# Spectral mixer and bilinear GLU on one core: products split out of their PSUM banks, weight sums on another engine, a new order at two seams

## The chip, the cores and the metric

One core of a Trainium2 chip. The metric is the device time of one execution in microseconds (us), lower is better; the kernel before took 715.27 us (median of three runs, 714.61 to 717.80).

## The reference

All of it is fp32, on a sequence of S = 2048 tokens of D = 640:

```python
h  = x + irfft2(rfft2(layernorm(x)) * (w_r + 1j*w_i))
z  = layernorm(h)
h2 = h + ((z @ w_gate) * (z @ w_up)) @ w_down      # F = 1728, no other nonlinearity
```

## The kernel before, in words

The first 194 us or so do the spectral part as matmuls with Fourier tables; the change does not touch them. The rest is the GLU, in two blocks of 1024 tokens. The 1728 columns of F are cut into 14 chunks of 128 (the last is half a chunk). A fp32 operand is split into a rounded high part, **hi** (written by ACT, ScalarE), and the rest, **lo** (source minus hi, written by VectorE = DVE or GpSimd = POOL); each product of two split operands is three matmuls: hi·hi, hi·lo, lo·hi. The accumulators `e` (gate and up) and `d` (down) are PSUM banks, four of each.

**Chunks.** A block starts with chunks 12 and 13, done plainly (`gu`, `gate_parts`: u copied by ACT, gate times up by DVE, then the split). Chunks 0 to 11 go in six *pairs* p = 0..5, chunk 2p (even) and 2p+1 (odd). `strassen` computes one chunk, gate and up over both halves of the tokens, by a Strassen scheme in seven products. I call them P1 to P7 in the order of the code; P1, P3 and P5 are 6 matmuls of 512 columns, P2, P4, P6 and P7 are 9. P1, P3, P5 and P7 go into bank `oa`, P2 and P4 into `ob`, P6 into `oc`. After P1, P2 and P3 ACT copies the bank to SBUF (`h0`, `c22`, `h1`; lines 971, 981, 985); DVE adds later banks to these copies (988, 991, 1004) and multiplies (992: `h1`; 1010: `h0`). So a chunk gives two finished tiles, `h0` and `h1`, gate times up for the two token halves.

**Down products.** The down projection of a finished pair is itself a Strassen scheme, over the four tiles of the pair (even chunk: a11 = `h0`, a21 = `h1`; odd chunk: a12 = `h0`, a22 = `h1`). It needs seven split operands, kept in `hop` (tile `ht`), slots 0 to 6: a11, a12, a22, a21+a22, a21+a22-a11, a11-a21 (`s3`), a12-(a21+a22-a11) (`s4`). `down_products` makes 28 products of 3 matmuls with 320 columns (84 in all), in ten groups g0 to g9 of 3, 3, 3, 2, 3 (twice over). Each is followed at once by a DVE addition to the output rows `x` (line 921). The first group holds p1a, p5a, p1b; the second p5b, p6a, p3a. p6a accumulates on the bank of p1a, so it waits until DVE has added p1a to `x`; p3a needs slot 6 (`s4`).

**Order.** It is written by hand. `strassen` calls `at(n)` behind product Pn; I say *slot n*. The groups of the pair before are hung into slots 2 to 7 of the even chunk (g0 to g5) and 1 to 4 of the odd one (g6 to g9), side jobs too. The next chunk's gate and up weights are prepared one chunk ahead (`prep`, `ahead[0..3]`: ACT copies 834 and 846, POOL rests 835 and 851, POOL sums 838 to 841), the down weights in five steps `wdn[0..4]` (`load_d`): `plain` at slot 3, `sums` at slot 6 and a further part at slot 7 of the even chunk, two more parts at slot 4 of the odd chunk. `sums` is four subtractions of 128x320 on DVE (588 to 591); the ACT copy of `wdn[2]` (line 580) waits for them.

Most of the change lies at the odd chunk's end. Behind P5 DVE adds to `c22`, multiplies `h1`, forms a21+a22 (995) and a21+a22-a11 (996) in SBUF, and `split` makes three lo's (939). Then come the additions and the product for `h0` (1004, 1010) and `s4` (1018). The splits of `s4` and `h0` (a12) are put off into the next chunk (`HELD["late"]`), behind its P1.

**Other pieces.** At a block's start chunks 12 and 13 run beside the preparation of the token sums (`t12`, `t34`), whose lo for `t3` is made by `lo()`, line 710. The first pair has the down products of chunks 12 and 13 in its slots instead (`down`, 10 matmuls for each j of 8: j = 0 to 3 in slots 2 to 5, two each in slots 6 and 7 of the even chunk; none in the odd one). In chunk 11 of the first block ACT also normalises the eight row tiles of the next block (line 645), all at slot 4.

Of the kernel before, what the change touches and what calls it, by code (L numbers as in the profile page):

```python
# [13 lines left out]
AF = mybir.ActivationFunctionType  # L14
OP = mybir.AluOpType

P = 128
# [21 lines left out]
def f32(ap):  # L39
    return ap.bitcast(F32)  # L40
# [29 lines left out]
def tile_spectral_glu(ctx: ExitStack, tc: tile.TileContext, x, wf, wgu, wlast, wdown, wdlast,  # L70
# [31 lines left out]
    def wk(shape, name):  # L102
        return work.tile(shape, F32, tag="wk", name=name)
# [464 lines left out]
    def load_d(p):  # L568
        w = home("dA" if p in (0, 2, 4) else "dB", [P, 2, 1280], "wd", F32R)
        raws = [wk([P, D], "draw") for _ in range(2)]  # L570
        if p >= 5:
            return split_in(("d", p), w, wdown[p] if p < 6 else wdlast, raws, nc.gpsimd)
        v = home("dC", [P, 2, 960], "wt", F32R)
        W["d", p] = w, v
        for i, r in enumerate(raws):
            nc.sync.dma_start(r, wdown[p][:, D * i:D * i + D])
        (r, q), sub = raws, OP.subtract

        def part(o, a, src, n):
            act(o[:, 0, a:a + n], src, AF.Copy)  # L580
            nc.gpsimd.tensor_tensor(o[:, 1, a:a + n], src, f32(o[:, 0, a:a + n]), op=sub)

        def plain():
            part(w, 0, r[:, 0:320], 320)
            part(w, 320, q, 640)

        def sums():
            tt(r[:, 0:320], r[:, 320:640], r[:, 0:320], op=sub)  # L588
            tt(r[:, 320:640], q[:, 320:640], r[:, 320:640], op=sub)
            tt(q[:, 320:640], q[:, 320:640], r[:, 0:320], op=sub)  # L590
            tt(q[:, 0:320], q[:, 0:320], q[:, 320:640], op=sub)
# [341 lines left out]

    HELD = {}

    def split(src, a, engine=None):
        hi, lo = (hop[:, a, l] for l in range(2))
        act(hi, src, AF.Copy)  # L938
        (engine or nc.vector).tensor_tensor(lo, src, f32(hi), op=OP.subtract)  # L939

    def strassen(c, blk, ahead, downs, side):
        wa, ws = W[c]
        p, odd = divmod(c, 2)

        def at(n):
            if downs.get(n):
                for f in downs[n]:
                    f()
                if c:
                    pop(1)  # L950
            for f in side.get(n, ()):
# [19 lines left out]
        act(h0, oa, AF.Copy)  # L971
# [19 lines left out]
        tt(c22, oa, c22, op=OP.add)  # L991
        tt(h1, h1, c22, op=OP.mult)  # L992
        if odd and p < 5:
            a11, a21 = HELD["a11"], HELD["a21"]
            tt(a21, a21, h1, op=OP.add)  # L995
# [3 lines left out]
        elif odd:  # L999
            split(h1, 4)  # L1000
        at(5)
        oc = single()
        product(oc, True, wa, 0, b21, [(wa, 256, b5[0])])
        tt(h0, oc, h0, op=OP.add)
        if ahead and not odd:
# [4 lines left out]
        tt(h0, oa, h0, op=OP.mult)  # L1010
        if not odd:
            HELD["a11"], HELD["a21"] = h0, h1
            if p < 5:
                nc.gpsimd.tensor_tensor(c22, h0, h1, op=OP.subtract)
                HELD["s3"] = c22
        elif p < 5:
            s4 = wk([P, 512], "s4")
            tt(s4, h0, c22, op=OP.subtract)
            HELD["late"] = [(s4, 6), (h0, 1)]
        at(7)  # L1020
        if c == 11:
            split(h0, 5)

    order = [6, 0, 1, 2, 3, 4, 5]
    steps = [(blk, p) for blk in range(2) for p in order]
# [1 line left out]
    for n, (blk, p) in enumerate(steps):  # L1027
        if p == 6:
            if blk == 0:
# [23 lines left out]
                hi, lo = t34(0)  # L1053
                hi()
                late()
                lo()
                wdn = load_d(p)
            else:
                copies, sums, high, low = prep(0, blk)
# [26 lines left out]
                    t_rest(j)  # L1086
                late()
                gu(NC - 1, 1)
                issue(wdn)
                for j in range(4):  # L1090
                    t1s[j][1]()
                late = gate_parts(NC - 1, 1)
                hi, lo = t34(0)
                hi()
                late()
                lo()
# [14 lines left out]
        wdn = load_d(p)  # L1111
        slots = [{}, {}]
        if prev[1] == 6:
            js = [[0], [1], [2], [3], [4, 5], [6, 7]]
            slots[0] = {n: [lambda j=j, prev=prev: down(*prev, j) for j in k] for n, k in enumerate(js, 2)}
        else:
            fs = down_products(*prev, (0, 1)) + down_products(*prev, (2, 3))
            slots[0] = dict(zip(range(2, 8), fs))
            slots[1] = dict(zip((1, 2, 3, 7 if p == 5 else 4), fs[6:]))
        for ci in range(2):  # L1120
            c = 2 * p + ci
            side = {n: [] for n in range(8)}
            ahead = None
            if c < 11:
                ahead = prep(c + 1, blk)
                if c < 10:
                    side[6 if ci else 7].append(lambda c=c: load_raw(c + 2))
            if p == 5:
                if ci == 0:
                    side[3].append(lambda wdn=wdn: issue(wdn))  # L1130
                else:
                    side[4].append(lambda: (split(HELD["a11"], 0, nc.gpsimd), split(HELD["a21"], 3)))
            elif ci == 0:
                side[3].append(wdn[0])
                side[6].append(wdn[1])
                side[7].append(wdn[2])
            else:
                def rest(wdn=wdn, ahead=ahead):
                    split(HELD["a11"], 0, nc.gpsimd)
                    ahead[2]()  # L1140
                    ahead[3]()
                    wdn[3]()
                    split(HELD["s3"], 5, nc.gpsimd)
                    wdn[4]()

                side[4].append(rest)
            if c == 11 and blk == 0:
                pop(len(fill))
                dj = load_direct(1, [wk([P, D], "draw"), stage[:, 0:640], stage[:, 640:1280]])
                side[1] += [lambda: issue(dj[0]), lambda: issue(dj[1]), lambda: load_raw(0)]  # L1150

                def low(ks):
# [142 lines left out]
```

## Time and profile before

| | us |
|---|---|
| runs: median (lowest to highest) | 715.27 (714.61 to 717.80) |
| the profiled execution, its own time | 717.91 |
| its span, first to last instruction | 716.0 |
| PE busy in the span | 687.9 (96%) |
| DVE / POOL / ACT busy | 539.5 / 363.2 / 312.1 |
| mean granted PE clock | 0.99 |

PE is busy 96% of the span, so the time is PE's work plus the gaps between its matmuls. In a timeline row the first number is the start from the span's start, the second how long the row lasts, then engine, line, output<-inputs and the count; in brackets stands the idle time ahead of it and what ended it. Matmuls overlap, so a group's true cost is read from one row's start to the next row's start, not from the duration.

### The profile page before, as it was taken

Reading aid. Unit: us, or ns where it says so; the run is one execution under the profiler, and the core shown is the slowest. Engines: PE = TensorE matmul, PEld = TensorE weight load, DVE = VectorE, ACT = ScalarE, POOL = GpSimd, SP = SyncE. Lnnn points to the kernel's source line nnn. Section 1 sums busy time; section 2 is a strip of 40 time slices with the busy share of each in tenths; the row PEclk is TensorE's granted clock in tenths of the full one; section 3 lists DMA queues with packets and bytes.
Section 4 is the critical chain, followed back from the end, with each engine's and each line's share of the span. In section 5 each row is a group of like instructions: output and inputs, shape, how many; then the busy total and the mean of one; then the engine's idle time right before and its main releaser. Section 6 shows DMA issues by size and latency. Waiting matters only on the chain.

```text
span 716.0 us, 10313 instructions
## 1 busy us (share of the span) xinstructions
PE 687.9 (96%) x3784; PEld 606.2 (85%) x3784; DVE 539.5 (75%) x1022; ACT 312.1 (44%) x605; POOL 363.2 (51%) x322
## 2 busy tenths in 40 slices
PE   8999999999999899999999999999799999999998
PEld 8989989887797688888888889888688888888888
DVE  7968886998866878787877667665778778686755
ACT  6966674475514234342425263433315243334310
POOL 3101114330368676768676714266766767768600
PEclk9999999999999999999999999999799999999999
DMA  9426771002211111121213113300212121211003
GB/s 336 174 94 201 229 224 52 0 1 75 74 37 42 38 44 63 38 73 38 75 37 92 38 43 148 105 8 30 74 38 74 38 74 38 74 38 57 18 1 148
DMA packets 21075, 55.07 MB, mean 77 GB/s; under 512 B 2336, under 2 KB 7200, under 8 KB 21024
## 3 DMA queue, kind: packets, MB, share of 16 engines
q1 hardware_dynamic: 20304, 52.53, 22.2%
q0 software_dynamic: 288, 1.48, 0.6%
q8 instruction: 30, 0.49, 0.3%
q10 hardware_dynamic: 432, 0.39, 0.2%
q14 instruction: 21, 0.17, 0.1%
HBM read 49.16 MB, written 5.24 MB: 76 GB/s over the span
## 4 chain that ended last, share of the span: by engine, by line
PE 69%; DVE 25%; ACT 3%; issue 2%; POOL 1%; DVEq 0%; ACTq 0%
PE e L109 32%; PE d L109 21%; DVE ht L939 5%; DVE h L995 2%; DVE h L992 2%; PE re L109 2%; PE im L109 2%; PE u L413 2%; PE im L455 2%; PE eo L109 2%; DVE c L996 2%; PE im L241 1%; PE re L282 1%; DVE c L991 1%; DVE h L1010 1%
## 5 line engine op out<-in xcount | busy, mean ns | idle before, releaser
L109 PE MATMUL e<-xt,wst 128*128 128x512 f32 x864 | 216.3, 395 | 0.0
L109 PEld LDWEIGHTS e<-xt,wst 128*128 128x128 f32 x864 | 162.2, 191 | 31.3
L109 PE MATMUL d<-wd,ht 128*128 128x320 f32 x832 | 147.7, 312 | 4.7 <-DVE ht L939 3.6
L921 DVE TENSOR_TENSOR x<-d,x 128x320 f32<-128x320 f32 x280 | 123.9, 483 | 37.6 <-PE d L109 33.4
L109 PEld LDWEIGHTS d<-wd,ht 128*128 128x128 f32 x832 | 131.6, 189 | 13.9 <-DVE ht L939 4.1
L835 POOL TENSOR_TENSOR wst<-raw,wst 128x1024 fp32r<-128x1024 f32 x23 | 55.3, 2406 | 99.0 <-ACT wst L834 83.0
L109 PE MATMUL d<-wt,ht 128*128 128x320 f32 x360 | 70.8, 314 | 13.0 <-DVE x L921 13.0
L109 PE MATMUL e<-t,wst 128*128 128x512 f32 x288 | 74.7, 395 | 0.9 <-ACT h L971 0.9
L109 PEld LDWEIGHTS d<-wt,ht 128*128 128x128 f32 x360 | 57.9, 189 | 17.8 <-DVE x L921 16.0
L851 POOL TENSOR_TENSOR wst<-raw,wst 128x896 fp32r<-128x896 f32 (+1 forms) x46 | 71.4, 1574 | 0.2 <-ACT wst L846 0.2
L109 PEld LDWEIGHTS e<-t,wst 128*128 128x128 f32 x288 | 53.0, 189 | 10.9 <-ACT h L971 1.5
L846 ACT ACTIVATE wst<-raw 128x896 fp32r<-128x896 f32 (+1 forms) x48 | 30.2, 677 | 45.7 <-POOL raw L840 44.9
L988 DVE TENSOR_TENSOR h<-e,h 128x512 f32<-128x512 f32 x24 | 16.6, 691 | 43.3 <-PE e L109 38.5
L938 ACT ACTIVATE ht<-h 128x512 fp32r<-128x512 f32 x48 | 29.8, 625 | 34.1 <-DVE h L992 19.0
L580 ACT ACTIVATE wd<-draw 128x320 fp32r<-128x320 f32 (+1 forms) x30 | 15.7, 558 | 66.2 <-DVE draw L588 66.2
L109 PE MATMUL e<-xt,wdir 128*128 128x512 f32 x180 | 42.1, 392 | 0.2 <-DVE ht L790 0.2
L484 POOL CAST qr<-bits 1x128 fp32r<-1x128 f32 x15 | 4.2, 280 | 71.4 <-DVE qr L488 71.4
L109 PEld LDWEIGHTS e<-xt,wdir 128*128 128x128 f32 x180 | 33.5, 188 | 7.5 <-issue 0.6
L896 DVE TENSOR_TENSOR x<-d,x 128x320 f32<-128x320 f32 x62 | 27.3, 484 | 13.3 <-PE d L109 13.3
L109 PE MATMUL e<-ht,wst 128*128 128x512 f32 x144 | 37.0, 392 | 0.0
L992 DVE TENSOR_TENSOR h<-h,c 128x512 f32<-128x512 f32 x24 | 35.5, 1479 | 0.8
L560 POOL TENSOR_TENSOR wd<-draw,wd 128x640 fp32r<-128x640 f32 x8 | 14.7, 1858 | 42.0 <-ACT wd L559 42.0
(206 smaller groups left out, 1260.5 us busy)
## 6 DMA issues: line engine op xcount, KB each, us to landing
raw<-in_wgu_dram SPq DMA_DIRECT2D x24, 640.0 KB, 3.8
wts<-in_wf_dram SPq DMA_DIRECT2D x16, 644.0 KB, 4.0
draw<-in_wdown_dram SPq DMA_DIRECT2D x24, 320.0 KB, 3.1
x<-in_x_dram SPq DMA_DIRECT2D x15, 320.5 KB, 5.6
out_dram<-x SPq DMA_DIRECT2D x15, 320.0 KB, 2.2
bits<-in_mm_dram SPq DMA_DIRECT2D x32, 128.0 KB, 3.9
raw<-in_wgu_dram SPq DMA_DIRECT2D x4, 320.0 KB, 3.9
draw<-in_wdlast_dram SPq DMA_DIRECT2D x4, 320.0 KB, 4.5
```

Source lines behind the costliest of these rows:

```text
L109: nc.tensor.matmul(o, l, r, start=start, stop=stop, skip_group_check=True)
L560: los.append(lambda r=r, a=a, b=b: engine.tensor_tensor(w[:, 1, a:b], r, f32(w[:, 0, a:b]), op=OP.subtract))
L580: act(o[:, 0, a:a + n], src, AF.Copy)
L835: ptt(wa[:, 1], stage[:, 0:1024], f32(wa[:, 0]), op=OP.subtract)
L846: act(ws[:, 0, o:o + b - a], stage[:, a:b], AF.Copy)
L851: ptt(ws[:, 1, o:o + b - a], stage[:, a:b], f32(ws[:, 0, o:o + b - a]), op=OP.subtract)
L896: tt(xv, ps[b][:, 0:320], xv, op=OP.add)
L921: tt(xv, o, xv, op=OP.add)
L938: act(hi, src, AF.Copy)
L939: (engine or nc.vector).tensor_tensor(lo, src, f32(hi), op=OP.subtract)
L988: tt(h1, ob, h1, op=OP.add)
L992: tt(h1, h1, c22, op=OP.mult)
```

## The change

1. Odd chunk: the gate-times-up tiles stay in their PSUM banks. P4's sum is added into `ob`, the product is made in `ob` (odd chunks), a21+a22 goes into bank `oc`, a21+a22-a11 is made in `ob` from the `s3` that POOL had formed, `s4` again in `ob`. hi and lo are taken from the banks. Slots 2, 3 and 4 are split behind P5 and P6, slots 1 and 6 behind P7, before the next chunk; nothing is put off any more. ACT makes one more copy (`h0` into `oc`, line 1027 of the new kernel).
2. The ten groups of down products sit in slots 1 to 7 of the even chunk (g0 to g6) and 2 to 4 of the odd one (g7 to g9; 1, 2 and 7 in pair 5). In pair 0 `down` j = 0 stands in slot 3 and 1, 2 in slot 4.
3. `sums` of the down weights runs on POOL.
4. At a block's start the lo's of chunk 12's gate are made before `t3`'s lo; in block 1 the copies of the down weights come after that of chunk 13's gate.
5. The eight normalisations in chunk 11 are spread: three in slot 3, two in 5, two in 6, one in 7. In pair 5 the lo of a21 goes to POOL, and chunk 11's `h0` is finished in bank `oa`.

```diff
         def sums():
-            tt(r[:, 0:320], r[:, 320:640], r[:, 0:320], op=sub)
...
+            gp = nc.gpsimd.tensor_tensor
+            gp(r[:, 0:320], r[:, 320:640], r[:, 0:320], op=sub)
...
+    def hi_of(src, a):
+        act(hop[:, a, 0], src, AF.Copy)
+    def lo_of(src, a, engine=nc.vector):
+        engine.tensor_tensor(hop[:, a, 1], src, f32(hop[:, a, 0]), op=OP.subtract)
+    def split(src, a):
+        hi_of(src, a)
+        lo_of(src, a, nc.gpsimd)
...
-        for src, a in HELD.pop("late", ()):
-            split(src, a)
...
-        tt(h1, ob, h1, op=OP.add)
+        tt(ob, ob, h1, op=OP.add)
...
-        tt(h1, h1, c22, op=OP.mult)
-        if odd and p < 5:
-            a11, a21 = HELD["a11"], HELD["a21"]
-            tt(a21, a21, h1, op=OP.add)
-            tt(c22, a21, a11, op=OP.subtract)
-            for src, a in ((h1, 2), (a21, 3), (c22, 4)):
-                split(src, a)
...
+        tt(ob if odd else h1, ob, c22, op=OP.mult)
+        if odd:
+            hi_of(ob, 2 if p < 5 else 4)
         at(5)
...
+        if odd and p < 5:
+            tt(oc, ob, HELD["a21"], op=OP.add)
+            hi_of(oc, 3)
+            lo_of(ob, 2)
+            tt(ob, ob, HELD["s3"], op=OP.subtract)
+            hi_of(ob, 4)
+            lo_of(oc, 3)
...
-            s4 = wk([P, 512], "s4")
-            tt(s4, h0, c22, op=OP.subtract)
-            HELD["late"] = [(s4, 6), (h0, 1)]
         at(7)
+        if odd and p < 5:
+            hi_of(h0, 1)
+            lo_of(ob, 4)
+            act(oc, h0, AF.Copy)
+            tt(ob, h0, ob, op=OP.subtract)
+            hi_of(ob, 6)
+            lo_of(oc, 1)
+            lo_of(ob, 6)
...
-                lo()
             gu(NC - 2, 1)
-            gate_parts(NC - 2, 1, wdn[0] if blk == 0 else ())()
-            for f in t34(1):
-                f()
+            g = gate_parts(NC - 2, 1, wdn[0] if blk == 0 else ())
+            rest = t34(1)
+            rest[0]()
+            g()
+            lo()
+            rest[1]()
...
-            js = [[0], [1], [2], [3], [4, 5], [6, 7]]
+            js = [[0], [1, 2], [3], [4, 5], [6, 7]]
...
-            slots[0] = dict(zip(range(2, 8), fs))
-            slots[1] = dict(zip((1, 2, 3, 7 if p == 5 else 4), fs[6:]))
+            slots[0] = dict(zip(range(1, 8), fs))
+            slots[1] = dict(zip((1, 2, 7) if p == 5 else (2, 3, 4), fs[7:]))
...
-                side[4].append(lambda: low(range(8)))
+                for n, ks in ((3, (0, 1, 2)), (5, (3, 4)), (6, (5, 6)), (7, (7,))):
+                    side[n].append(lambda ks=ks: norms(ks))
```

How it moves instructions, at three places. **DVE, from P5 of chunk 3 to the first additions of chunk 4.** `e_...` are PSUM banks, `h0`, `h1`, `c22`, `s4` SBUF tiles, `ht` holds `hop`. Before:

```order
L991 TENSOR_TENSOR c22_2513<-e_2473,c22_2513 128x512
L992 TENSOR_TENSOR h1_2534<-h1_2534,c22_2513 128x512
L995 TENSOR_TENSOR h1_2351<-h1_2351,h1_2534 128x512
L996 TENSOR_TENSOR c22_2513<-h1_2351,h0_2304 128x512
L939 TENSOR_TENSOR ht_1757<-h1_2534,ht_1757 128x512
L939 TENSOR_TENSOR ht_1757<-h1_2351,ht_1757 128x512
L939 TENSOR_TENSOR ht_1757<-c22_2513,ht_1757 128x512
L1004 TENSOR_TENSOR h0_2480<-e_2596,h0_2480 128x512
L1010 TENSOR_TENSOR h0_2480<-e_2473,h0_2480 128x512
L1018 TENSOR_TENSOR s4_2618<-h0_2480,c22_2513 128x512
L939 TENSOR_TENSOR ht_1757<-s4_2618,ht_1757 128x512
L939 TENSOR_TENSOR ht_1757<-h0_2480,ht_1757 128x512
```

After (the additions to `x` follow):

```order
L995 TENSOR_TENSOR c22_2513<-e_2487,c22_2513 128x512
L996 TENSOR_TENSOR e_2503<-e_2503,c22_2513 128x512
L1002 TENSOR_TENSOR h0_2494<-e_2589,h0_2494 128x512
L1004 TENSOR_TENSOR e_2589<-e_2503,h1_2365 128x512
L941 TENSOR_TENSOR ht_1757<-e_2503,ht_1757 128x512
L1007 TENSOR_TENSOR e_2503<-e_2503,c22_2343 128x512
L941 TENSOR_TENSOR ht_1757<-e_2589,ht_1757 128x512
L1017 TENSOR_TENSOR h0_2494<-e_2487,h0_2494 128x512
L941 TENSOR_TENSOR ht_1757<-e_2503,ht_1757 128x512
L1028 TENSOR_TENSOR e_2503<-h0_2494,e_2503 128x512
L941 TENSOR_TENSOR ht_1757<-e_2589,ht_1757 128x512
L941 TENSOR_TENSOR ht_1757<-e_2503,ht_1757 128x512
```

Twelve operations in both; the sum into `h0` (P6) has moved ahead of the pair's sums and lo's, and in each new row one operand is a bank.

**PE, the same seam**, from P6 of chunk 3; `wd`, `wt` are down weights, `d_...` the down banks. Before:

```order
L109 MATMUL e_2596<-xt_1177,wst_2310 128x512 x9
L109 MATMUL e_2473<-xt_1177,wst_2310 128x512 x9
L109 MATMUL e_2626<-xt_1177,wst_2482 128x512 x6
L109 MATMUL e_2646<-t12_1856,wst_2482 128x512 x6
L109 MATMUL e_2646<-xt_1177,wst_2482 128x512 x3
L109 MATMUL d_2658<-wd_2291,ht_1757 128x320 x3
L109 MATMUL d_2663<-wd_2291,ht_1757 128x320 x3
L109 MATMUL d_2668<-wd_2291,ht_1757 128x320 x3
L109 MATMUL e_2626<-t12_1856,wst_2482 128x512 x6
L109 MATMUL d_2682<-wd_2291,ht_1757 128x320 x3
L109 MATMUL d_2658<-wt_2294,ht_1757 128x320 x3
```

After:

```order
L109 MATMUL e_2589<-xt_1177,wst_2310 128x512 x9
L109 MATMUL e_2487<-xt_1177,wst_2310 128x512 x9
L109 MATMUL e_2630<-xt_1177,wst_2496 128x512 x6
L109 MATMUL d_2646<-wd_2295,ht_1757 128x320 x3
L109 MATMUL d_2651<-wd_2295,ht_1757 128x320 x3
L109 MATMUL d_2656<-wd_2295,ht_1757 128x320 x3
L109 MATMUL e_2662<-t12_1856,wst_2496 128x512 x6
L109 MATMUL e_2662<-xt_1177,wst_2496 128x512 x3
L109 MATMUL d_2674<-wd_2295,ht_1757 128x320 x3
L109 MATMUL d_2646<-wt_2298,ht_1757 128x320 x3
```

g0 now stands ahead of P2, and P3 no longer stands between g0 and p6a, the first product that uses a down bank again (`d_2658` before, `d_2646` after).

**POOL, the end of chunk 2**, `draw` being raw down weights. After (before, the rows of lines 589 to 592 are not there):

```order
L852 TENSOR_TENSOR wst_2310<-raw_1854,wst_2310 128x896
L852 TENSOR_TENSOR wst_2310<-raw_1854,wst_2310 128x256
L589 TENSOR_TENSOR draw_2296<-draw_2296 128x320
L590 TENSOR_TENSOR draw_2296<-draw_2297,draw_2296 128x320
L591 TENSOR_TENSOR draw_2297<-draw_2297,draw_2296 128x320
L592 TENSOR_TENSOR draw_2297<-draw_2297 128x320
L1021 TENSOR_TENSOR c22_2343<-h0_2308,h1_2365 128x512
L581 TENSOR_TENSOR wd_2295<-draw_2296,wd_2295 128x320
L836 TENSOR_TENSOR wst_2496<-raw_1854,wst_2496 128x1024
```

The four sums stand between the rests of the next chunk's weights and `s3`.

More of the change, by code (lines that the diff above doesn't have):

```diff
@@ L934, in tile_spectral_glu @@
     HELD = {}
[L936 to L939, printed above, removed]
+    def hi_of(src, a):
[5 more added lines that the diff above has]
+        lo_of(src, a, nc.gpsimd)
     def strassen(c, blk, ahead, downs, side):
@@ L1004, in strassen @@
         tt(h0, oc, h0, op=OP.add)
+        if odd and p < 5:
[5 more added lines that the diff above has]
+            lo_of(oc, 3)
+        elif odd:
+            lo_of(ob, 4)
         if ahead and not odd:
@@ L1009, in strassen @@
         product(oa, False, wa, 640, t4, [(wa, 896, b5[0])])
-        tt(h0, oa, h0, op=OP.mult)
+        tt(oa if c == 11 else h0, oa, h0, op=OP.mult)
         if not odd:
@@ L1015, in strassen @@
                 HELD["s3"] = c22
-        elif p < 5:
-            s4 = wk([P, 512], "s4")
-            tt(s4, h0, c22, op=OP.subtract)
-            HELD["late"] = [(s4, 6), (h0, 1)]
         at(7)
-        if c == 11:
-            split(h0, 5)
+        if odd and p < 5:
+            hi_of(h0, 1)
+            lo_of(ob, 4)
+            act(oc, h0, AF.Copy)
[3 more added lines that the diff above has]
+            lo_of(ob, 6)
+        elif odd:
+            hi_of(oa, 5)
+            lo_of(oa, 5)
     order = [6, 0, 1, 2, 3, 4, 5]
@@ L1092, in tile_spectral_glu @@
                 late = gate_parts(NC - 1, 1)
+                issue(wdn)
                 hi, lo = t34(0)
@@ L1113, in tile_spectral_glu @@
         if prev[1] == 6:
-            js = [[0], [1], [2], [3], [4, 5], [6, 7]]
-            slots[0] = {n: [lambda j=j, prev=prev: down(*prev, j) for j in k] for n, k in enumerate(js, 2)}
+            js = [[0], [1, 2], [3], [4, 5], [6, 7]]
+            slots[0] = {n: [lambda j=j, prev=prev: down(*prev, j) for j in k] for n, k in enumerate(js, 3)}
         else:
             fs = down_products(*prev, (0, 1)) + down_products(*prev, (2, 3))
-            slots[0] = dict(zip(range(2, 8), fs))
-            slots[1] = dict(zip((1, 2, 3, 7 if p == 5 else 4), fs[6:]))
+            slots[0] = dict(zip(range(1, 8), fs))
+            slots[1] = dict(zip((1, 2, 7) if p == 5 else (2, 3, 4), fs[7:]))
         for ci in range(2):
@@ L1131, in tile_spectral_glu @@
                 else:
-                    side[4].append(lambda: (split(HELD["a11"], 0, nc.gpsimd), split(HELD["a21"], 3)))
+                    side[4].append(lambda: (split(HELD["a11"], 0), split(HELD["a21"], 3)))
             elif ci == 0:
-                side[3].append(wdn[0])
-                side[6].append(wdn[1])
-                side[7].append(wdn[2])
+                for n, i in ((3, 0), (6, 1), (7, 2)):
+                    side[n].append(wdn[i])
             else:
                 def rest(wdn=wdn, ahead=ahead):
-                    split(HELD["a11"], 0, nc.gpsimd)
+                    split(HELD["a11"], 0)
                     ahead[2]()
@@ L1142, in rest @@
                     wdn[3]()
-                    split(HELD["s3"], 5, nc.gpsimd)
+                    split(HELD["s3"], 5)
                     wdn[4]()
@@ L1150, in tile_spectral_glu, with norms @@
                 side[1] += [lambda: issue(dj[0]), lambda: issue(dj[1]), lambda: load_raw(0)]
-                def low(ks):
+                def norms(ks):
                     for k in ks:
```

10 lines of the change are left out of this document (3 added, 7 removed).

## The prediction

> **What bounds the kernel now.** I read the page first (PE 96% busy, so only its gaps can be won), then the waits, then the timeline at the places that they name, and last the chain, for the pitch of the pairs. PE's longest wait:
>
> ```profile
> PE d L109 <- DVE x L921: 13.6, 12, 3.2
> ```
>
> Twelve times (13.6 us, the longest 3.2) a down product waits until DVE has added an earlier product to `x`, which frees the down bank. PE's timeline around the seam of chunks 3 and 4 shows where:
>
> ```profile
> 266.27 5.60 PE L109 MATMUL e<-xt,wst 128*128 128x512 f32 x24
> 271.71 1.52 PE L109 MATMUL e<-t,wst 128*128 128x512 f32 x6
> ...
> 273.75 1.48 PE L109 MATMUL d<-wd,ht 128*128 128x320 f32 x9
> 275.07 1.55 PE L109 MATMUL e<-t,wst 128*128 128x512 f32 x6
> 276.45 0.60 PE L109 MATMUL d<-wd,ht 128*128 128x320 f32 x3
> 277.97 0.70 PE L109 MATMUL d<-wt,ht 128*128 128x320 f32 x3 [0.92 <-DVE x L921]
> ```
>
> From start to start, 6 matmuls of 512 columns take 1.38 us (275.07 to 276.45) and 3 of 320 columns 0.44 (a third of 273.75 to 275.07). So p6a could start at 276.89 and starts at 277.97: 1.08 lost. What DVE does meanwhile:
>
> ```profile
> 266.47 0.69 DVE L991 TENSOR_TENSOR c<-e,c 128x512 f32<-128x512 f32 x1 [0.63 <-PE e L109]
> 267.20 1.32 DVE L992 TENSOR_TENSOR h<-h,c 128x512 f32<-128x512 f32 x1
> 268.63 1.61 DVE L995 TENSOR_TENSOR h<-h,h 128x512 f32<-128x512 f32 x1
> ...
> 271.45 1.28 DVE L939 TENSOR_TENSOR ht<-h,ht 128x512 fp32r<-128x512 f32 x2
> ...
> 274.04 0.69 DVE L1010 TENSOR_TENSOR h<-e,h 128x512 f32<-128x512 f32 x1
> 274.83 0.69 DVE L1018 TENSOR_TENSOR s<-h,c 128x512 f32<-128x512 f32 x1
> 276.22 0.69 DVE L939 TENSOR_TENSOR ht<-s,ht 128x512 fp32r<-128x512 f32 x1 [0.70 <-ACT ht L938]
> ...
> 277.43 1.28 DVE L921 TENSOR_TENSOR x<-d,x 128x320 f32<-128x320 f32 x3
> ```
>
> DVE is busy nearly all the time and comes to the first addition only at 277.43; PE goes on 0.54 later. Operations on two SBUF tiles take 1.32 and 1.61 there, those with a bank as operand 0.69. The size of that seam comes from the chain, which passes P4 of every even chunk:
>
> ```profile
> 239.23 3.31 PE e L109 x9
> ...
> 279.14 2.06 PE e L109 x9
> ...
> 394.00 2.06 PE e L109 x9
> ...
> 514.51 3.84 PE e L109 x9
> ...
> 554.52 2.06 PE e L109 x9
> ...
> 669.12 2.06 PE e L109 x9
> ```
>
> A pair is 108 matmuls of 512 columns (18 times 1.38 = 24.8) and 84 of 320 (28 times 0.44 = 12.3), 37.1 at most; the 24 in a row above give 24.5, so I take 37.0. The three pitches from 279.14 to 394.00 are 114.86, 3.9 too long; the three from 554.52 to 669.12 are 114.60, 3.6 too long. The pitches after the first seam of a block, 239.23 to 279.14 and 514.51 to 554.52, are 39.9 and 40.0, 2.9 and 3.0 too long. The first seam itself (pair 0 to pair 1) is worse, in both blocks:
>
> ```profile
> 228.51 0.84 PE L109 MATMUL e<-xt,wst 128*128 128x512 f32 x3
> ...
> 237.73 0.71 PE L109 MATMUL d<-wt,ht 128*128 128x320 f32 x3 [3.19 <-DVE x L921]
> ...
> 239.03 1.48 PE L109 MATMUL e<-xt,wst 128*128 128x512 f32 x3
> ...
> 503.33 0.84 PE L109 MATMUL e<-xt,wst 128*128 128x512 f32 x3
> ...
> 514.31 4.04 PE L109 MATMUL e<-xt,wst 128*128 128x512 f32 x9
> ...
> 503.33:514.51 11.18, 7.21 (x29) 6.00 (x28) 9.95 (x13) 4.86 (x9) 6.23 (x4) 0.71 0.39 118
> ```
>
> Between the rows lie 9 matmuls of 512 and 18 of 320 columns, 4.7 us; they take 10.52 and 10.98, so 5.8 and 6.3 are lost. Part of that is clock: the last row is the stage by windows, with a granted clock of 0.71, and nine matmuls take 4.04 there instead of 2.06. **All ten seams together lose 3.9 + 3.6 + 2.9 + 3.0 + 5.8 + 6.3 = 25.5 us.**
>
> **Part 1 and 2: banks in place, and the order at the seam.** An operation with a bank costs 0.69 (266.47, 274.04). One on two SBUF tiles can cost the same, as at the end of chunk 11, where POOL has nothing to do; at the seam POOL works beside it. ACT makes a hi out of a bank in 0.60:
>
> ```profile
> 418.93 0.69 DVE L992 TENSOR_TENSOR h<-h,c 128x512 f32<-128x512 f32 x1
> ...
> L785 ACT ACTIVATE ht<-e 128x512 fp32r<-128x512 f32 x4 | 2.4, 600 | 9.6 <-DVE e L784 9.6
> ```
>
> I lay out the new seam from T, the end of P5 (266.27 in the rows above). By the rows above, DVE starts 0.2 after PE's last matmul (266.27, 266.47), a DVE operation that needs the one ahead of it 0.73 to 0.79 after that one's start (266.47, 267.20; 274.04, 274.83), one that does not 0.6 (two in 1.28); between ACT and DVE I allow 0.04. DVE: `c22` 0.2; product 0.95; P6's sum 2.3 (P6 ends at 2.06); a21+a22 3.0; lo 3.6; minus `s3` 4.2; lo 4.9; P7's product 5.5; lo 6.1; `s4` 6.7. ACT then makes the hi of `s4` from 7.4 to 8.0; DVE fills the time with the lo of a12 at 7.3, makes the lo of `s4` at 8.05, and the first addition to `x` starts at 8.65. Before it started at T + 11.16. PE may go on 0.54 later, at T + 9.2. PE for its part: P6, P7, P1 5.44; g0 now directly behind, 1.32; P2 2.04; p5b 0.44: it wants p6a at T + 9.24. p3a, 0.44 later, needs the second addition (9.1 to 9.6) and the lo of `s4` (8.75): both there. So the gap goes, by a margin of about nothing; I charge 0.15 a seam, 1.5 for ten. p5a uses slot 3, ready at 5.5, and runs at 5.9. The operation with no row is ACT's copy from SBUF into a bank (as DVE's writes into one other than its source): by the nearest rows between 0.60 and 0.68 (640 wide, SBUF to SBUF, two in 1.35, below); a copy by 0.08 slower delays nothing, as DVE is busy till 7.3. I take 0.6.
>
> At the first seam of a block DVE has the same list; the odd chunk has no down products, so nothing is queued ahead of it, and the stages by windows above have it busy 9.95 of 11.18. Slots 0 and 5 stay POOL's, made from the odd chunk's slot 4 on as before, a whole chunk tail ahead of their use. The stall gone, PE's clock should stay up. So I take the whole seam there too.
>
> A rule speaks against this. The Trainium skill, Perfetto Trace Analysis, section Optimizing Scalar/DVE Operations, gives DVE about 60 ns of access per instruction on SBUF and about 125 on PSUM; on eight operations of the new list that would be 0.5 us a seam, and 5 us over ten seams on the result. The rows do not show it: 0.69 on two SBUF tiles (418.93) and 0.69 with a bank (266.47).
>
> **Part 3: weight sums on POOL.** DVE loses four rows of about 0.5 in each pair, beside PE's work: worth nothing by itself. POOL's rows in chunk 4, from its first to `s3`:
>
> ```profile
> 277.74 2.42 POOL L835 TENSOR_TENSOR wst<-raw,wst 128x1024 fp32r<-128x1024 f32 x1 [6.76 <-ACT wst L834]
> ...
> 281.05 1.03 POOL L839 TENSOR_TENSOR raw<-raw 128x384 f32<-128x384 f32 x1
> ...
> 286.03 3.29 POOL L851 TENSOR_TENSOR wst<-raw,wst 128x896 fp32r<-128x896 f32 x2
> 292.74 1.29 POOL L1014 TENSOR_TENSOR c<-h,h 128x512 f32<-128x512 f32 x1 [3.42 <-DVE h L1010]
> ```
>
> A sum 384 wide takes 1.03, so four of 320 at most 4.1; POOL idles 3.4 ahead of `s3`, and starts 1.9 earlier than now, because ACT's weight copy is no longer behind the late splits: it comes behind the hi of `s4` (8.0) and the copy of P1 (0.6), so POOL starts near T + 9.6 instead of 277.74 = T + 11.5. It did 11.6 of work before the idle time, so the sums end at T + 25.3. Behind them ACT waits with the weight part (0.5) and, queued behind it, chunk 5's copy of P1, which P3 there needs at T + 30 (18 matmuls of P6 and P7 4.1, chunk 4 12.4, its 20 down products 8.8, P1, P2 and g7 4.8). 3.6 us of room: nothing is lost.
>
> **Part 4 and 5: the block changes.** PE and the engines it waits for at block 0's first pair, and last PE behind chunk 11:
>
> ```profile
> 191.16 1.33 PE L109 MATMUL d<-wd,ht 128*128 128x320 f32 x8
> ...
> 194.20 0.97 PE L109 MATMUL e<-t,wst 128*128 128x512 f32 x3 [0.68 <-ACT h L971]
> ...
> 188.81 2.67 DVE L710 SCALAR_TENSOR_TENSOR ht<-bt,ht 128x512 fp32r<-128x512 f32 x2
> ...
> 188.22 1.35 ACT L559 ACTIVATE wd<-draw 128x640 fp32r<-128x640 f32 x2
> 192.12 0.60 ACT L785 ACTIVATE ht<-e 128x512 fp32r<-128x512 f32 x1 [2.54 <-DVE e L784]
> ...
> 193.56 0.59 ACT L971 ACTIVATE h<-e 128x512 f32<-128x512 f32 x1
> ...
> 425.19 1.00 PE L109 MATMUL d<-wd,ht 128*128 128x320 f32 x5 [0.62 <-DVE x L921]
> ```
>
> Ten down matmuls from 191.16 (1.47) should end at 192.63; P3 starts at 194.20, 1.57 late, because ACT's copy of P1 (193.56) stands behind the gate's hi (192.12), which waits for DVE's product behind the 2.67 of `t3`'s lo. With the product at 188.81 that hi starts at 189.6, behind ACT's two weight copies, and 2.03 later, as now, the copy is done: 191.6. P3, now directly behind P2, wants it at 191.16; 0.45 stays, gain 1.1. Its down products come 1.4 later, so POOL's rest of their weights, now the first wait there, is covered. Behind chunk 11 ACT's hi of a22 stands behind eight normalisations, DVE behind that, and PE 0.62 behind DVE; spread, the hi comes with its product: gain 0.6. At block 1's start the two weight copies move behind the gate: between nothing and their 1.35; they are ready long before P1 ends, so I take 0 and keep 1.35 for the range. Freed buffers come round one allocation sooner, behind readers in the odd chunk's slot 4: 0.
>
> **The sum.** 25.5 - 1.5 + 1.1 + 0.6 = 25.7 us. The profiled execution took 717.91 (span 716.0 and 1.9 around it), so 692.2 on its own scale; it lies 2.6 above the median of 715.27, which would give 689.6. Some of the 2.6 may be half clock that the other runs did not have and so cannot win; I take the middle, rounded down a little, **690.5 us**.
>
> **The rivals.**
> *The seams only shrink (0.21).* The chain above has no margin. If it ends 0.5 to 1 us later (ten hand-overs between three engines stand in it, and 0.05 to 0.1 more at each is enough), ten gaps of that size remain: 5 to 10 less the 1.5 charged, 694 to 699, say 696. For it: DVE's 0.70 wait for ACT at 276.22, a hand-over of the same kind. The Trainium skill's figure for PSUM above would land here too, near 694; the two rows of 0.69 speak against it, and 0.03 of the 0.21 is for it.
> *POOL's sums hold up ACT, and PE behind it (0.04): slower than before.* Decides when the four sums take 3.6 longer than 4.1, near 2 us each; from there each us costs 1 in each of ten pairs, and at 2.6 each the whole gain is gone; at 3 each it is 43 us lost, 733 us. Against it: POOL's 1024-wide row takes 2.42, three times the width.
> *It moves the wait, not the time (0.03).* If PE waited next for something equally late, such as slot 6, the time would stay at 715. Against it: every step at the seam comes at least 2 us earlier.
>
> **How the numbers follow.** Forecast 0.72 with 687.5 to 693; the seams-shrink case reaches to 699. The range 687.5 to 699 leaves out the two last rivals and the ends. The lower end is all gaps gone, with the median's scale (25.5 + 1.6 + 0.6 = 27.7 off 715.27: 687.6). About 0.5%, 3.6 us, is what a measurement of this kernel can tell: faster 0.93 (both first cases), same 0.03, slower 0.04.
>
> **What would show it.** Right: in the pair pitch of the chain 37.0 to 37.3 instead of 38.2; no wait of PE for DVE's `x` over 0.3 at the seams; DVE's operations at the odd chunk's end at 0.69 each; no granted clock under 1 near 239 or 508. Wrong: a pitch of 38, PE waiting for ACT's hi or for POOL, or ACT waiting for the weight sums beyond P3 of an odd chunk.

## The result and the profile after

The changed kernel takes 691.83 us (median of four runs, 691.79 to 692.10) against 715.39 (four runs, 714.61 to 717.80): a ratio of 0.9666, 95% interval 0.9643 to 0.9689. Its profiled execution took 692.10 (span 690.3), 25.8 less than that of before (717.91). 690.5 was predicted, in a range of 687.5 to 699.

The page, and PE's waits, the two that answer to the 13.6 us for `x` of before (us in total, times, longest):

```profile
PE 679.8 (98%) x3784; PEld 602.3 (87%) x3784; DVE 478.3 (69%) x980; ACT 318.8 (46%) x615; POOL 383.4 (56%) x364
```

```profile
PE d L109 <- DVE x L922: 0.6, 3, 0.2
...
PE e L109 <- ACT h L977: 0.2, 1, 0.2
```

The same seam as before, chunk 3 to 4, on PE's timeline. T, the end of P5, is 258.29 here:

```profile
258.29 5.60 PE L109 MATMUL e<-xt,wst 128*128 128x512 f32 x24
263.73 1.48 PE L109 MATMUL d<-wd,ht 128*128 128x320 f32 x9
265.05 1.55 PE L109 MATMUL e<-t,wst 128*128 128x512 f32 x6
266.43 0.84 PE L109 MATMUL e<-xt,wst 128*128 128x512 f32 x3
267.11 0.60 PE L109 MATMUL d<-wd,ht 128*128 128x320 f32 x3
267.57 0.68 PE L109 MATMUL d<-wt,ht 128*128 128x320 f32 x3
```

There is no bracket in it: p6a (267.57) starts 0.46 after p5b, 0.02 more than three matmuls of 320 need. And DVE's list beside it:

```profile
258.49 0.69 DVE L995 TENSOR_TENSOR c<-e,c 128x512 f32<-128x512 f32 x1 [0.63 <-PE e L109]
259.22 0.70 DVE L996 TENSOR_TENSOR e<-e,c 128x512 f32<-128x512 f32 x1
...
262.53 0.69 DVE L1007 TENSOR_TENSOR e<-e,c 128x512 f32<-128x512 f32 x1
263.13 0.68 DVE L941 TENSOR_TENSOR ht<-e,ht 128x512 fp32r<-128x512 f32 x1
263.73 0.68 DVE L1017 TENSOR_TENSOR h<-e,h 128x512 f32<-128x512 f32 x1
...
266.94 1.28 DVE L922 TENSOR_TENSOR x<-d,x 128x320 f32<-128x320 f32 x3
```

Each operation costs 0.68 to 0.70, where before they cost 0.69 to 1.61, and the first addition to `x` starts at T + 8.65 instead of T + 11.16. The pitch, by P4 of the even chunks on the chain:

```profile
271.38 2.06 PE e L109 x9
...
383.13 2.06 PE e L109 x9
...
496.34 2.06 PE e L109 x9
...
644.74 2.06 PE e L109 x9
```

Four pitches in the second block are 148.40, 37.10 each (38.2 before). Three in the first are 111.75, 37.25: one seam has a gap of 0.46. Last the clock (the third number from the end of a windows row), at the second block's first seam. Before, the 11.18 us that end with P4 of pair 1 had 7.21 of PE work and a clock of 0.71; now the 11.18 us that end with the same product (496.34 above) have 10.96 of PE work and the full clock:

```profile
485.16:496.34 11.18, 10.96 (x58) 9.55 (x57) 9.52 (x18) 7.37 (x14) 9.28 (x7) 1.00 0.35 119
```

### The profile page after: what moved, and what is told of

Same layout as the page of the kernel before. It is cut to its first block, busy times and chain, and to the rows that moved or that the text cites. A ratio compares the mean times of both kernels' runs of the same rounds, so it can differ in the third digit from the quotient of the medians.

```text
span 690.3 us, 10276 instructions
## 1 busy us (share of the span) xinstructions
PE 679.8 (98%) x3784; PEld 602.3 (87%) x3784; DVE 478.3 (69%) x980; ACT 318.8 (46%) x615; POOL 383.4 (56%) x364
## 4 chain that ended last, share of the span: by engine, by line
PE 81%; DVE 11%; ACT 4%; POOL 2%; issue 1%; ACTq 0%; DVEq 0%
PE e L109 41%; PE d L109 23%; PE re L109 2%; PE im L109 2%; PE u L413 2%; PE im L455 2%; PE eo L109 2%; PE im L241 2%; DVE ht L941 1%; PE re L282 1%; POOL wst L836 1%; PE ir L455 1%; PE y L109 1%; ACT wst L847 1%; DVE x L631 1%
## 5 line engine op out<-in xcount | busy, mean ns | idle before, releaser
L109 PE MATMUL e<-xt,wst 128*128 128x512 f32 x864 | 213.1, 390 | 0.0
L109 PEld LDWEIGHTS e<-xt,wst 128*128 128x128 f32 x864 | 159.9, 188 | 30.7
L109 PE MATMUL d<-wd,ht 128*128 128x320 f32 x832 | 145.1, 309 | 0.3 <-DVE x L922 0.2
L836 POOL TENSOR_TENSOR wst<-raw,wst 128x1024 fp32r<-128x1024 f32 x23 | 56.8, 2472 | 70.9 <-ACT wst L835 68.1
L852 POOL TENSOR_TENSOR wst<-raw,wst 128x896 fp32r<-128x896 f32 (+1 forms) x46 | 65.1, 1438 | 0.2 <-ACT wst L847 0.2
L992 DVE TENSOR_TENSOR e<-e,h 128x512 f32<-128x512 f32 x24 | 16.8, 700 | 47.0 <-PE e L109 34.1
L977 ACT ACTIVATE h<-e 128x512 f32<-128x512 f32 x24 | 14.3, 595 | 74.7 <-PE e L109 74.7
L938 ACT ACTIVATE ht<-e 128x512 fp32r<-128x512 f32 x44 | 26.3, 597 | 37.3 <-DVE e L996 14.2
L580 ACT ACTIVATE wd<-draw 128x320 fp32r<-128x320 f32 (+1 forms) x30 | 15.6, 555 | 50.3 <-POOL draw L589 50.0
L941 DVE TENSOR_TENSOR ht<-e,ht 128x512 fp32r<-128x512 f32 x54 | 37.0, 685 | 2.0 <-ACT ht L938 1.6
L560 POOL TENSOR_TENSOR wd<-draw,wd 128x640 fp32r<-128x640 f32 x8 | 12.4, 1569 | 46.1 <-ACT wd L559 46.1
```

The source lines that it names most:

```text
L109: nc.tensor.matmul(o, l, r, start=start, stop=stop, skip_group_check=True)
L836: ptt(wa[:, 1], stage[:, 0:1024], f32(wa[:, 0]), op=OP.subtract)
L852: ptt(ws[:, 1, o:o + b - a], stage[:, a:b], f32(ws[:, 0, o:o + b - a]), op=OP.subtract)
L938: act(hop[:, a, 0], src, AF.Copy)
L941: engine.tensor_tensor(hop[:, a, 1], src, f32(hop[:, a, 0]), op=OP.subtract)
L992: tt(ob, ob, h1, op=OP.add)
```

## The experiments

Eleven kernels, each the changed kernel (691.8) with something undone or added; all compute the same. The kernel before ran beside them at 716.85, 717.73 and 717.26 (medians of 12, 7 and 7 runs, 713.6 to 718.4). It scatters by 5 us, the changed kernel by 0.3, so the third column is the better measure; but the changed kernel did not run beside them, its 691.8 is that of the result above.

| kernel | us | over 691.8 | ratio to before, 95% |
|---|---|---|---|
| sums_on_dve | 692.35 | 0.5 | 0.9635 to 0.9696 |
| sbuf_tiles | 720.33 | 28.5 | 1.0038 to 1.0075 |
| banks_old_order | 707.47 | 15.6 | 0.9844 to 0.9906 |
| old_slots | 699.23 | 7.4 | 0.9731 to 0.9792 |
| block_edits_undone | 699.74 | 7.9 | 0.9726 to 0.9791 |
| block_edits_and_slots | 694.29 | 2.5 | 0.9664 to 0.9706 |
| seam_plus_one | 698.49 | 6.7 | 0.9714 to 0.9775 |
| pool_six_more | 697.71 | 5.9 | 0.9696 to 0.9770 |
| pool_twelve_more | 754.78 | 63.0 | 1.0502 to 1.0557 |
| first_seams_stall | 702.80 | 11.0 | 0.9773 to 0.9835 |
| first_seams_three | 698.35 | 6.5 | 0.9718 to 0.9766 |

**The weight sums.**

```diff
-            gp = nc.gpsimd.tensor_tensor
+            gp = tt
```

> The changed kernel with one part undone: the four weight sums of a pair run on DVE again. Theory (the seam list of DVE is what the change wins): the sums lie in the even chunk, behind P6, where DVE has 2 us to spare and PE waits for nothing; 691.8 plus or minus 1. Rival (DVE had too much to do in a pair, and every row taken from it counts): four rows of 0.5 us in ten pairs, so 20 us come back, about 712.

692.35: the sums are worth about half a microsecond, little more than the runs scatter. The rival falls: no 20 us came back, so DVE's share of the span was not the limit.

**The operands' place.** The order of the change, but in SBUF (the even chunk's product, too, reads two SBUF tiles again):

```diff
-        tt(ob, ob, h1, op=OP.add)
+        tt(h1, ob, h1, op=OP.add)
...
-        tt(ob if odd else h1, ob, c22, op=OP.mult)
+        tt(h1, h1, c22, op=OP.mult)
         if odd:
+            ob = h1
...
         if odd and p < 5:
+            oc = wk([P, 512], "s4")
```

> The changed kernel with its new order, but at an odd chunk's end the sums and splits work on SBUF tiles, as before, and not in PSUM banks. Theory (price of the operands): the operations that run while POOL still works, up to about T + 5, cost 1.3 to 1.6 instead of 0.69; three to five of them make the first addition to x 2 to 3.5 us late, with no margin, so 20 to 35 us more over ten seams: 712 to 727. Rival 1 (the order at the seam is what won): 692 to 695. Rival 2 (an access to PSUM costs DVE 0.06 us more than one to SBUF): some 0.5 us less a seam, 687 to 691.

720.33, inside the theory's 712 to 727 and no faster than the kernel before; both rivals fall. DVE and POOL in that seam show why (T is 263.26):

```profile
267.22 1.78 DVE L941 TENSOR_TENSOR ht<-h,ht 128x512 fp32r<-128x512 f32 x1
269.04 1.25 DVE L1009 TENSOR_TENSOR h<-h,c 128x512 f32<-128x512 f32 x1
270.21 0.68 DVE L941 TENSOR_TENSOR ht<-s,ht 128x512 fp32r<-128x512 f32 x1
```

```profile
266.71 1.74 POOL L941 TENSOR_TENSOR ht<-c,ht 128x512 fp32r<-128x512 f32 x1
268.42 1.32 POOL L581 TENSOR_TENSOR wt<-draw,wt 128x320 fp32r<-128x320 f32 x1
```

The same line 941 on two SBUF tiles takes 1.78 while POOL works and 0.68 once POOL has ended (269.74). With a bank as one operand DVE keeps its 0.68 to 0.70 beside POOL too, as at 262.53 in the changed kernel, where POOL works the whole time:

```profile
262.47 0.87 POOL L581 TENSOR_TENSOR wt<-draw,wt 128x320 fp32r<-128x320 f32 x1
```

In the GLU part of that profile all 150 such operations (three operands of 512 columns, one input a bank) that start while POOL works take 0.68 to 0.70; the 57 of sbuf_tiles on two SBUF tiles that do so take 0.76 to 2.33. So the bank is not cheaper in itself; it keeps DVE out of POOL's way. The Trainium skill, SBUF — State Buffer, section Who interferes with whom, states the same: a DVE instruction with two SBUF inputs contends with a GpSimd instruction that reads SBUF, and one with at most one SBUF input does not, unless it runs in a mode that uses both of DVE's port pairs. PE then waits for the splits at every seam:

```profile
PE d L109 <- DVE ht L941: 18.0, 10, 3.5
```

So it is not the late addition to `x` alone, as the theory had it: in the seam above PE stands 1.36 us for a split and 0.46 for `x`. Behind the two longest stalls (3.5) the clock falls as well, which is some 3.4 of the 28.5.

**The order.** Banks, in the order of before:

```diff
         if odd:
             hi_of(ob, 2 if p < 5 else 4)
+        if odd and p < 5:
+            a21 = HELD["a21"]
+            tt(a21, ob, a21, op=OP.add)
+            hi_of(a21, 3)
+            lo_of(ob, 2)
+            tt(ob, ob, HELD["s3"], op=OP.subtract)
+            hi_of(ob, 4)
+            lo_of(a21, 3)
+            lo_of(ob, 4)
         at(5)
...
+            HELD["late"] = [(ob, 6), (h0, 1)]
```

> The changed kernel with banks, but in the order of before: a21+a22 and its splits stand ahead of P6's sum on DVE, and the splits of s4 and a12 come behind the next chunk's P1. Two splits read SBUF tiles (a21+a22 is written in place in SBUF, a12 stays there). Theory (prices first, order second): by the rows of the seam the first addition to x starts at T + 9.85 instead of T + 8.65, so 1.2 us at each of ten seams, about 704. Rival (the banks alone do it): 692 to 694. Rival (the order alone does it): 712 or more.

707.47, between the rivals, 3.5 over the theory. In the seam (T = 260.36) the first addition starts at T + 9.61:

```profile
267.40 0.70 DVE L1030 TENSOR_TENSOR e<-h,e 128x512 f32<-128x512 f32 x1
268.76 0.69 DVE L941 TENSOR_TENSOR ht<-e,ht 128x512 fp32r<-128x512 f32 x1 [0.66 <-ACT ht L938]
269.37 0.68 DVE L941 TENSOR_TENSOR ht<-h,ht 128x512 fp32r<-128x512 f32 x1
269.97 1.28 DVE L922 TENSOR_TENSOR x<-d,x 128x320 f32<-128x320 f32 x3
```

DVE now stands idle for ACT's hi of `s4` (0.66); the new order puts the lo of a12 into that hole. PE's waits for `x` are 10.9 us in all, ten times; the first seam of each block has two more gaps, of 0.97 and 0.51, which I had not counted and which make up most of the 3.5.

**The slots.**

```diff
-            js = [[0], [1, 2], [3], [4, 5], [6, 7]]
+            js = [[0], [1], [2], [3], [4, 5], [6, 7]]
...
-            slots[0] = dict(zip(range(1, 8), fs))
+            slots[0] = dict(zip(range(2, 8), fs))
```

(and the rest of the table with it)

> The changed kernel with the down products back in their old slots (g0 behind P2 of the even chunk, ten groups over slots 2 to 7 and 1 to 4; the eight of a block's first pair over slots 2 to 7). Theory: p6a is then wanted 1.38 us later (behind P3), so the seam has 1.4 us of margin instead of none, and nothing is lost elsewhere but the copy of P1 in block 0's first pair (0.5 to 1.1 at one place): 691 to 693. Rival (the moved groups are part of the gain, as they cover a wait of PE behind P1): 5 us or more come back, 697 or more.

699.23: my theory fell, the rival held. The wait, and PE and DVE at the seam (T = 258.28):

```profile
PE e L109 <- DVE h L1017: 7.5, 10, 1.1
```

```profile
258.28 5.60 PE L109 MATMUL e<-xt,wst 128*128 128x512 f32 x24
264.55 1.62 PE L109 MATMUL e<-t,wst 128*128 128x512 f32 x6 [0.66 <-DVE h L1017]
```

```profile
263.72 0.68 DVE L1017 TENSOR_TENSOR h<-e,h 128x512 f32<-128x512 f32 x1
```

P2 of the next chunk waits for the product with P7 (line 1017). Before, P2 started at 271.71, 2.3 us ahead of that product (274.04): its bank had long been free. Now `ob` and `oc` are held to the seam's end, so by the code the bank that comes free first is P7's. P2 comes 0.82 late; g0 in slot 1 puts 1.32 us of other work there. The move of the groups is the other half of working in the banks.

**The block changes.** Parts 4 and 5 back in the old order:

```diff
-            g = gate_parts(NC - 2, 1, wdn[0] if blk == 0 else ())
-            rest = t34(1)
-            rest[0]()
-            g()
-            lo()
-            rest[1]()
+            gate_parts(NC - 2, 1, wdn[0] if blk == 0 else ())()
+            for f in t34(1):
+                f()
...
-                for n, ks in ((3, (0, 1, 2)), (5, (3, 4)), (6, (5, 6)), (7, (7,))):
-                    side[n].append(lambda ks=ks: norms(ks))
+                side[4].append(lambda: norms(range(8)))
```

> The changed kernel with Parts 4 and 5 undone: the gates and the splits of t3 in their old order at both block changes, the eight normalisations behind chunk 11's slot 4 in one piece, block 1's weight copies ahead of the gate. Theory (1.1 at block 0's first pair and 0.6 behind chunk 11, nothing at block 1's start): 693.5, 693 to 694.2. Rival 1 (the old order costs nothing any more): 691.8. Rival 2 (block 1's copies count too, 1.35): 694.9.

699.74: far over all three. PE at block 0's first pair, and the stage by windows:

```profile
190.09 0.84 PE L109 MATMUL e<-xt,wst 128*128 128x512 f32 x3
193.81 2.93 PE L109 MATMUL e<-t,wst 128*128 128x512 f32 x6 [2.88 <-ACT h L977]
```

```profile
193.00:200.00 7.00, 6.19 (x18) 5.47 (x19) 2.10 (x4) 3.88 (x8) 4.91 (x5) 0.51 0.01 2
```

P3 waits 3.0 for ACT's copy of P1, because the ten down matmuls that stood between P2 and P3 before (1.47) are no longer there, and PE runs the next 7 us at half clock. (One run of the four, 698.19, had a mean granted clock of 1.0, the others 0.995: without the half clock it is 1.5 less.) At block 1's start, where I had counted nothing, P3 comes 1.9 late. To separate the two changes I put those down products back as well:

```diff
-            js = [[0], [1, 2], [3], [4, 5], [6, 7]]
-            slots[0] = {... enumerate(js, 3)}
+            js = [[0], [1], [2], [3], [4, 5], [6, 7]]
+            slots[0] = {... enumerate(js, 2)}
```

> The kernel with Parts 4 and 5 undone, and also the eight down products of each block's first pair back in their old slots (the first of them behind P2, ahead of P3). Theory (in the old order ACT's copy of P1 is late for P3, and the ten down matmuls that stood between P2 and P3 covered 1.5 us of that): at block 0 1.1 more than in the changed kernel, at block 1 nothing, behind chunk 11 0.9; no half clock near 193; 693.8, 693.3 to 694.5. Rival (the old order of the gates costs the whole 7.9 us by itself): 699 to 700.

694.29, in the theory's range: the old order alone costs 2.5, and the rest of the 7.9 came from taking the down products away from it.

**The margin.**

```diff
             lo_of(oc, 1)
             lo_of(ob, 6)
+            lo_of(ob, 6)
```

> The changed kernel with one more DVE operation of 0.6 to 0.69 in each of ten seams, ahead of the first addition to x (the lo of s4 is made twice; the result is the same). Theory (the seam has no margin: p6a comes as soon as the addition allows): each seam 0.6 to 0.69 longer, 6 to 7 in all, 698 to 699. Rival (PE is not bound by DVE there, and there is room): 692 to 693.

698.49. PE at the seam, with the same T of 258.29, and DVE's first addition:

```profile
267.11 0.60 PE L109 MATMUL d<-wd,ht 128*128 128x320 f32 x3
268.30 0.68 PE L109 MATMUL d<-wt,ht 128*128 128x320 f32 x3 [0.59 <-ACT c L985]
```

```profile
267.67 1.28 DVE L922 TENSOR_TENSOR x<-d,x 128x320 f32<-128x320 f32 x3
```

Addition and p6a are both 0.73 later (266.94, 267.57). The bracket names an ACT copy that ended at about the same time; but the changed kernel's p6a started before that copy did, so the addition decides. The seam has no margin: what is added to DVE's list there is added to the time, 6.7 us over ten seams.

**POOL's room.**

```diff
+            for _ in range(6):
+                gp(r[:, 0:320], r[:, 320:640], r[:, 0:320], op=sub)
             gp(r[:, 0:320], r[:, 320:640], r[:, 0:320], op=sub)
```

> The changed kernel with six more sums of 320 columns on POOL in each of ten pairs, ahead of the four (the first one done seven times, six of them undoing each other), 0.96 each, so 5.8 us more a pair. By the prediction's account of the room (3.6 us behind the last sum): 2.2 us lost a pair, 22 in all, 714. By the trace of the changed kernel: ACT's weight part waits only for the first sum, which may end 7.5 us later before chunk 5's copy of P1 is late for P3; POOL's rests behind it fit into its 6.5 us of idle time a pair: 692 to 694.

697.71, neither: 0.6 us a pair. It is lost at the next seam: ACT's copy of gate and up weights (849) waits for POOL's sums of them (843), which now come later; the hi of the product stands behind it on ACT, and DVE for that (T = 259.12):

```profile
259.83 1.26 ACT L849 ACTIVATE wst<-raw 128x896 fp32r<-128x896 f32 x2 [4.97 <-POOL raw L843]
```

```profile
263.11 0.70 DVE L1006 TENSOR_TENSOR e<-e,h 128x512 f32<-128x512 f32 x1 [1.06 <-ACT ht L940]
```

With twelve (`range(12)`):

> The changed kernel with twelve more sums of 320 columns on POOL in each of ten pairs (11.5 us a pair; they undo each other). With six (5.8 us) 0.6 us a pair were lost, because ACT's weight copy waited for POOL and the hi of the next seam behind ACT. Theory (POOL has about 5.2 us of room a pair, and beyond it each us on POOL costs one on the end): 6.3 us a pair, 63 in all, 750 to 758. Rival (other engines take up part of it, POOL's late work being needed later than it now comes): 700 to 735.

754.78, as the theory had it, and slower than the kernel before. Now PE's wait is the one that the prediction's slower rival named, P3 behind ACT's copy of P1 behind the weight part that waits for the sums:

```profile
ACT wd L580 <- POOL draw L591: 162.8, 10, 17.0
...
PE e L109 <- ACT h L979: 34.4, 11, 4.3
```

The size fits by luck: the mean granted clock of that run is 0.971, and 0.029 of its 752.9 us is 22. PE stood for 5 of the 44 us at half clock, where the clock costs nothing, so some 20 of the 63 us lost are half clock, behind stalls of 2.2 to 4.3 us. The waits alone are some 43 us, 0.7 for each us on POOL beyond the room.

**The clock.**

```diff
             lo_of(ob, 6)
+            for _ in range(5 if p == 0 else 0):
+                lo_of(ob, 6)
```

> The changed kernel with five more DVE operations (the lo of s4 made six times) at the first seam of each block alone, so that PE stalls there for about 3.2 us more, as it did before the change. Theory 1 (such a stall lets PE's clock fall to half for some us): a granted clock of 0.5 for 3 to 10 us behind each stall, and 6.4 + 2 times 1.7 to 5 us: 701 to 708. Theory 2 (the clock fell for another reason): granted clock 1.0 throughout, 6.4 us more, 698.

702.80, theory 1. The stall of 4.0 us at 229.76, by windows, and what follows it:

```profile
229.50:234.50 5.00, 1.15 (x8) 0.92 (x8) 4.83 (x10) 1.54 (x2) 3.56 (x3) 1.00 0.18 73
234.50:238.50 4.00, 4.00 (x15) 3.45 (x14) 2.34 (x6) 1.14 (x3) 2.10 (x4) 0.57 0.00 0
238.50:242.50 4.00, 4.00 (x23) 3.54 (x22) 2.65 (x7) 1.59 (x3) 4.00 (x3) 1.00 0.00 0
```

The middle row has 0.57: 3.4 of its 4.0 us at one half, 1.7 us lost. Two stalls 3.6 longer than in the changed kernel and twice 1.7 give 10.7; 11.0 was measured. With three operations (`range(3 ...)`), a stall of 2.55:

> The changed kernel with three more DVE operations (not five) at the first seam of each block alone: a stall of PE of 2.6 us (0.38 and three times 0.73). Stalls of 1.5 and 1.9 left the granted clock at 1, those of 3.0 to 4.0 were followed by 3.4 or 6.8 us at 0.5. Without the fall of the clock: 691.8 + 4.4 = 696.2. With one stretch of 3.4 us behind each: 699.6.

698.35, but its runs spread from 697.43 to 699.36. The profiled one, 699.36, has the half clock behind both stalls:

```profile
232.00:236.00 4.00, 3.35 (x11) 3.06 (x12) 3.38 (x9) 0.00 (x0) 3.77 (x4) 0.57 0.00 0
```

So a stall of 2.55 may or may not bring it down: the mean granted clocks of the four runs are 0.994 to 0.998, two stretches of half clock or one. Over all profiles of this case, by PE's idle time in the GLU part: none of the 13 stalls of 1.2 to 1.4 us brought the clock down, all 18 of 2.2 or more that began at the full clock did, and of three of 1.7 to 1.8 one did. That one is in the kernel before, ahead of its longer stall of block 1, so the 1.9 that the last expectation calls harmless is not safe:

```profile
506.68 0.85 PE L109 MATMUL d<-wd,ht 128*128 128x320 f32 x4 [1.78 <-DVE ht L939]
...
512.55 1.17 PE L109 MATMUL d<-wt,ht 128*128 128x320 f32 x3 [2.19 <-DVE x L921]
```

```profile
504.00:508.00 4.00, 2.22 (x13) 1.86 (x12) 4.00 (x4) 0.14 (x1) 3.37 (x3) 1.00 0.54 177
508.00:518.50 10.50, 8.31 (x25) 6.68 (x24) 5.80 (x12) 5.13 (x9) 5.87 (x6) 0.51 0.15 47
```

The clock is down from 508.0 on, 1.3 us behind the first stall; the second falls into the half clock. The Trainium skill, TensorE: Matmul & The Clock Gate, section Why this matters for your kernels, advises no idle gap of PE beyond some 3 us; the rows agree in kind, and put the edge lower, near 2.

## Why the prediction was right, point by point

- *What bounds it, and the 25.5 us of the ten seams.* Right. The pitch went from 38.2 to 37.1, and PE's wait for `x` from 13.6 to 0.6. One reading was off without changing the sum: the 2.9 and 3.0 behind the first seams are not all seam, as P4 takes 3.31 and 3.84 there instead of 2.06; 1.3 and 1.8 of them are half clock.
- *The half clock inside that sum.* I counted the first seams whole, 5.8 + 6.3, with "the stall gone, PE's clock should stay up". Right, and shown by adding the stall back. How much it was, by a window of the kernel before and the row of 508.00 above:

```profile
238.00:242.00 4.00, 4.00 (x14) 3.37 (x14) 2.54 (x7) 1.37 (x3) 3.77 (x4) 0.57 0.00 0
```

  0.43 of 4.0 is 1.7. In the second stretch PE worked 8.31 of the 10.50 us, and 0.49 of that is 4.1: together 5.8 of the 25.8 us. The second stretch is three times as long, and unlike the first it has PE standing idle in it (2.19).
- *A bank operand at 0.69, the list ending at T + 8.65, PE wanting p6a at T + 9.24.* Right to some hundredths: 0.68 to 0.70, T + 8.65, T + 9.28. The 1.5 charged for ten seams came out as 1.2 (0.38 at each first seam, 0.46 at one other). The rule that spoke against it (the Trainium skill, Perfetto Trace Analysis, section Optimizing Scalar/DVE Operations: some 60 ns of access on SBUF, 125 on PSUM), by whose figures I had estimated 5 us, is not seen: 0.68 for two SBUF tiles (270.21 in sbuf_tiles), 0.68 with a bank (263.13).
- *"Margin about nothing", and the rival that seams only shrink.* The rival did not come, but the margin was as stated: 0.73 more on DVE made p6a 0.73 later at the seam shown, 6.7 us later in all.
- *"Freed buffers come round one allocation sooner ...: 0", and g0 in slot 1 counted only as making PE want p6a earlier.* The result is 0, the reason was wrong. The held banks make P2 wait for P7's product, 0.82 a seam; g0 in slot 1 hides it. I should have asked who hides it: by itself this term was 7.4.
- *Block changes: 1.1 + 0.6 + 0.* 1.7 in sum against 2.5 measured, and not in these parts: behind chunk 11 the gap that came back was 0.9, and at block 1's start, counted as nothing, it was 0.4, or 1.9 with the down products moved away. The order of the gates and the move of the down products need each other, which I had not seen.
- *Sums on POOL: 0, room 3.6.* The 0 is right (0.5 measured). The room was read off the wrong wait: ACT needs only the first sum, and the first thing to come late is the next seam, at about 5.2 us (six more sums, 5.8, lost 0.6). "From there each us costs 1" is too much for the wait alone (0.7) and came out only with the clock's part. The rival's place and sign came true at twelve more sums.
- *The scale.* This was the main miss in the total. The sum gave 25.7, the profiled executions differ by 25.8; on their scale 692.2 was forecast and 692.1 came. I then took the middle between that and the median's scale, 690.5, since half of the 2.6 between them might be half clock that other runs lacked. But it is the kernel before that scatters (713.6 to 718.4, at mean granted clocks of 0.990 to 0.998); the changed one, without its stalls, has one time. So what a run of before took for half clock falls away in every run, and the sum should have been taken off the profiled execution alone. Half clock is only part of that scatter: the runs of before at 0.990 took 715.6 to 717.9, those at the higher 0.993 took longer, 716.7 to 718.4. What the rest is stays open.

The parts undone one by one cost 0.5, 28.5, 15.6, 7.4 and 7.9, 60 us in all for a gain of 24. They don't add up: sbuf_tiles and banks_old_order undo the same part in two ways, and one part covers another's waits, as the block changes show (7.9, or 2.5 with the down products moved back as well).

## What to carry to other kernels

Where DVE is late beside a busy POOL, look first at the operations that read two SBUF tiles: one operand left in its PSUM bank takes them out of POOL's way. But a bank held longer delays whoever gets it next, so the same edit needs other work put ahead of that matmul. And count a PE stall of some 2 us or more at its length plus, in most runs, 1.7 us of half clock, or more where PE stops again within it.

## What was not expected of the hardware

- The half clock comes in pieces of 3.4 us. In the GLU part of the profiles 14 stretches are one piece long, and PE stands idle for at most 0.53 us in each; the five longer ones (6.8, and 10.2 once in the kernel before) have 0.7 to 2.2 us of idle time in them. So of two stalls of like length one can cost 1.7 us and another 3 or 4. That the idle time is what adds the pieces is read from these rows; no run tests it.
- A DVE operation on two SBUF tiles beside POOL is not slower by a fixed factor, but by what POOL's operation has left: the one at 267.22 ended at 269.00, 0.55 after the POOL operation (266.71 to 268.45) that it had run into, and of the 57 in sbuf_tiles 55 end 0.54 to 0.55 after theirs. POOL pays too: its rest of 640 columns took 2.02 in sbuf_tiles (the first row), 1.57 in pool_six_more, where DVE works in the banks (the second):

```profile
264.73 2.02 POOL L581 TENSOR_TENSOR wt<-draw,wt 128x640 fp32r<-128x640 f32 x1
```

```profile
264.62 1.57 POOL L581 TENSOR_TENSOR wt<-draw,wt 128x640 fp32r<-128x640 f32 x1
```
